# Attention and gated FFN on one core: the order of TensorE, ScalarE and VectorE taken from a list schedule

## The chip, the core and the metric

The kernel runs on one core of a Trainium2 chip. The core has TensorE (PE: matrix products, into the eight banks of PSUM), ScalarE (ACT: exponential, tanh, copies), VectorE (DVE: elementwise work and copies), GpSimd (POOL, here only the issuer of the loads) and SyncE (SP, here the issuer of the first small loads and of the stores). Each engine takes its instructions in the order in which the program gives them to it and waits at semaphores for the others. The metric is the device time of one execution in microseconds, lower is better.

## The reference

Sparse attention over 4 batches, 8 heads, 768 positions and a head size of 64, followed by a gated feed-forward network (512 to 1536 to 512) over the 3072 tokens, whose rows `x` are the heads' results side by side:

```python
    scores = scale * np.matmul(q, k.transpose(0, 1, 3, 2))
...
    mask = np.abs(blk_i - blk_j) <= window
    mask = mask | (blk_i == 0) | (blk_j == 0) | (blk_i == n_blocks - 1) | (blk_j == n_blocks - 1)
...
    scores = np.where(mask, scores, -1000000000.0)
    scores = scores - np.max(scores, axis=-1, keepdims=True)
    attn = np.exp(scores)
    attn = attn / (np.sum(attn, axis=-1, keepdims=True) + 1e-09)
    return np.matmul(attn, v).astype(np.float32)
...
    gate = 1.0 / (1.0 + np.exp(-(x @ w_gate)))
    val = x @ w_val
    return (gate * val @ w_out).astype(np.float32)
```

The mask is in blocks of 32 positions; three further blocks in each row of blocks come from the input `sampled_blocks`.

## The kernel before

A **unit** is one batch `b` with 256 of its 768 query positions (`u` = 0 to 2); there are 12, `n` = 0 to 11. A unit has four **pairs** of heads (`p`) and each pair three **steps** (`j`), of 256 key positions each. A step is `qk` (four score matmuls into `st`, two PSUM banks), `exp` on ACT (`pt<-st`, line 235) and `mul` on DVE with the 0/1 mask (line 239). After three steps a pair's `pv` multiplies with v, extended by a column of ones, so that the row sums come along (24 matmuls, line 257); `norm` divides by them on DVE (lines 267 and 269, giving `x16`), and `xt` transposes the result on PE and copies it into `xT` (lines 279 and 282).

The FFN of a unit has 12 column blocks `f`: eight matmuls into one bank `pg` (gate and value, line 295), tanh on ACT (`th`, line 305) and the gate on DVE (`ht`, line 306). Then `y` multiplies `ht` with `w_out`, 12 matmuls for each half of the unit (`py`, line 323), ACT copies the result to SBUF (line 332) and SP stores it.

A batch must be prepared: k, q and v are loaded in 16 bits (`k16`, `q16`, `v16`, two buffers each, for even and odd batches) by DMAs that POOL issues. For each pair and each of k and q, `pair_copy` gathers the two heads on DVE (`pr`, line 188), `pair_turn` transposes on PE (`tpq`, line 197) and copies into `kT` or `qT` (lines 202 and 204); `vcopy` copies v into `vex` (line 207).

All order is written out by hand: the main loop, from line 438, gives each unit six slots (`sl`), and a slot two steps. Slots 2 to 5 carry three `f` blocks each of the FFN of unit n−1, slots 0 and 1 the two `y` halves of unit n−2. `extra_copy` at a slot's end and `extra_pe` in the next slot put in one copy and one transpose of the next batch, from its list `pairs`, which is filled in each batch's second unit. Unit 0 has a loop of its own (from line 401), step by step, without an FFN. PSUM's eight banks are two score buffers of two banks and four single banks under the tag `m`, handed out in turn.

Of the kernel before, what the change touches and what calls it, by code (L numbers as in the profile page):

```python
# [14 lines left out]
ALU = mybir.AluOpType  # L16
# [13 lines left out]
NU = S // UQ  # L30

# [5 lines left out]
def _det_block_mask() -> np.ndarray:  # L37
    qb = np.arange(NB)[:, None]
    kb = np.arange(NB)[None, :]
    m = (np.abs(qb - kb) <= 1) | (qb == 0) | (kb == 0) | (qb == NB - 1) | (kb == NB - 1)  # L40
    return m.astype(np.float32)


@with_exitstack
def kernel(
# [87 lines left out]
    for j in range(3):  # L133
        load_wo(j)
    for r in range(2):
        nc.vector.memset(vex[r][:, :, :, D : D + 1], 1.0)
# [5 lines left out]
    def mask_blocks():  # L142
# [14 lines left out]
    def mask_rows():  # L157
        for c0, c1 in ((0, 512), (512, S)):
            p24 = ps.tile([NB, 512], f32, tag="m", bufs=4, name="p24")
            nc.tensor.matmul(  # L160
                p24[:, 0 : c1 - c0], mb16, e24[:, c0:c1], start=True, stop=True
            )
            nc.vector.tensor_copy(mb24[:, c0:c1], p24[:, 0 : c1 - c0])

    def mask_tile(c0, c1, t, eng):
        n = c1 - c0
        pm = ps.tile([128, 512], f32, tag="m", bufs=4, name="pm")
        w = 512 // n
        for i in range(w):
            nc.tensor.matmul(  # L170
                pm[:, i * n : (i + 1) * n],
                e24[:, (t + i) * 128 : (t + i + 1) * 128],
                mb24[:, c0:c1],
# [3 lines left out]
        dst = mask[:, t : t + w, c0:c1]  # L177
        src = pm.rearrange("a (w n) -> a w n", w=w)
        if eng is nc.scalar:
            nc.scalar.copy(dst, src)  # L180
        else:
            nc.vector.tensor_copy(dst, src)


    def pair_copy(src, b, p, t0=0, t1=NT):

        pr = work.tile([128, NT, 2, D], f16, tag="pr", bufs=4, name="pr")
        nc.vector.tensor_copy(  # L188
            pr[:, t0:t1, :, :],
            src[b % 2][:, 2 * p : 2 * p + 2, t0:t1, :].rearrange("a h t d -> a t h d"),  # L190
        )
        return pr

    def pair_turn(pr, dst, b, p, t0=0, t1=NT, eng=None):
        tp = ps.tile([128, 1024], f16, tag="m", bufs=4, name="tpq")
        for t in range(t0, t1):
            nc.tensor.transpose(  # L197
                tp[:, (t - t0) * 128 : (t - t0 + 1) * 128], pr[:, t, :, :], ident
            )
        d_ = dst[b % 2][:, p, t0 * 128 : t1 * 128]  # L200
        if eng is nc.scalar:
            nc.scalar.copy(d_, tp[:, 0 : (t1 - t0) * 128])  # L202
        else:
            nc.vector.tensor_copy(d_, tp[:, 0 : (t1 - t0) * 128])  # L204

    def vcopy(b, p):
        nc.vector.tensor_copy(
            vex[b % 2][:, 2 * p : 2 * p + 2, :, 0:D],
            v16[b % 2][:, 2 * p : 2 * p + 2, :, :],
        )  # L210

    class Step:


        def __init__(self, b, u, p, j):
            self.b, self.u, self.p, self.j = b, u, p, j

        def qk(self):
            b, u, p = self.b, self.u, self.p
            self.st = ps.tile([128, 2, 2, UQ], f32, tag="s", bufs=2, name="st")  # L220
            for i in range(2):
                t = 2 * self.j + i
                for a in range(2):
                    o = a * D
                    nc.tensor.matmul(  # L225
                        self.st[:, a, i, :],
# [6 lines left out]
        def exp(self):  # L233
            self.pt = work.tile([128, 2, 2, UQ], f16, tag="P", bufs=12, name="pt")
            nc.scalar.activation(self.pt, self.st, AF.Exp, bias=0.0, scale=SCALE)  # L235

        def mul(self):
# [8 lines left out]
    class Pair:  # L246


        def __init__(self, b, u, p, steps, xT):
            self.b, self.u, self.p, self.steps, self.xT = b, u, p, steps, xT  # L250

        def pv(self):
# [268 lines left out]
```

## Time and profile before

| | |
|---|---|
| time, median of 3 runs | 344.76 us (344.62 to 345.37) |
| the profiled execution | 344.88 us, span of its profile 343.1 us |
| ACT | 210.3 us busy, 323 instructions |
| DVE | 220.4 us busy, 531 instructions |
| loads issued by POOL | 14.16 MB as written, in 27.6% of the DMA engines' time over the span |

The page of a profile gives the busy time of each engine, the span in slices, the chain of work that ended last, and groups of instructions by line. Below, rows of the page's groups read: line, engine, operation, what it writes and reads, shapes, count, then busy microseconds and mean nanoseconds of one, then the idle time just before them and what ended it. Rows of an engine's timeline read: start and length in microseconds, engine, line, operation, count, and in brackets how long the engine had sat idle before and what it waited for. Rows of windows read: the stretch, its length, busy microseconds (and instructions) of PE, PE's weight loads, DVE, ACT and POOL, the granted clock of PE, the mean busy share of the DMA engines, and GB/s.

### The profile page before, as it was taken

The page shows a single profiled execution, that of the slowest core. Times are in us where ns is not written, and L with a number is a line of the kernel's source. Part 1 is how long each engine was busy: PE and PEld are TensorE (multiplying, and loading weights), DVE is VectorE, ACT ScalarE, POOL GpSimd, SP SyncE. Part 2 cuts the span into 40 slices and gives each one's busy share as a digit, 9 for nine tenths or more (in the row PEclk, how much of TensorE's full clock was granted, in tenths as well). Part 3 has the DMA queues.
Part 4 walks back from the last instruction along what each step waited for, and adds up shares of the span by engine and source line. Part 5 has one row for each costly group of instructions (what it writes and reads, how often), then busy time and mean ns, then how long its engine had stood idle before and what let it go on. Part 6 is the DMA issues. An engine that isn't in the chain of part 4 may idle for free.

```text
span 343.1 us, 8102 instructions
## 1 busy us (share of the span) xinstructions
PE 308.3 (90%) x3470; PEld 221.2 (64%) x3470; DVE 220.4 (64%) x531; ACT 210.3 (61%) x323; POOL 26.0 (8%) x37
## 2 busy tenths in 40 slices
PE   2788459899999999899999998999999999999995
PEld 1234237666858757657858766758768768678682
DVE  3655635777766757776767767767757757667240
ACT  1656325556867765656767856557867778677241
POOL 8834200003000000000000000000000000000000
PEclk9999658999999999999999999999999999999999
DMA  8999999509900000000000010000010010000101
GB/s 98 187 202 204 206 204 204 88 3 172 168 31 32 3 31 32 2 32 33 0 32 33 2 61 2 2 32 33 0 60 6 2 61 2 31 34 3 61 2 61
DMA packets 23215, 21.03 MB, mean 61 GB/s; under 512 B 2164, under 2 KB 20108, under 8 KB 23180
## 3 DMA queue, kind: packets, MB, share of 16 engines
q0 software_dynamic: 19472, 14.16, 27.6%
q1 hardware_dynamic: 3708, 6.37, 5.0%
q8 instruction: 27, 0.44, 0.5%
q14 instruction: 8, 0.07, 0.1%
HBM read 28.39 MB, written 6.29 MB: 101 GB/s over the span
## 4 chain that ended last, share of the span: by engine, by line
PE 76%; DMA 12%; DVE 6%; ACT 2%; POOL 2%; issue 1%; POOLq 0%
PE pg L295 36%; PE py L323 18%; PE pv L257 10%; PE st L225 6%; DMA q<-in_q_dram 6%; DMA wg<-in_moe_w_gate_dram 4%; PE tpq L197 3%; DVE pr L188 2%; DMA k<-in_k_dram 2%; DVE ht L306 2%; PE tpx L279 1%; DVE xT L282 1%; ACT pt L235 1%; ACT th L305 1%; DVE pt L239 1%
## 5 line engine op out<-in xcount | busy, mean ns | idle before, releaser
L235 ACT ACTIVATE pt<-st 128x1024 f16<-128x1024 f32 x144 | 144.5, 1022 | 14.4 <-PE st L225 13.1
L239 DVE TENSOR_TENSOR pt<-pt,mask 128x1024 f16<-128x1024 f16 x144 | 99.1, 690 | 49.1 <-ACT pt L235 49.0
L305 ACT ACTIVATE th<-pg 128x256 f32<-128x256 f32 x144 | 55.4, 385 | 59.1 <-PE pg L295 57.0
L295 PE MATMUL pg<-xT,wg 128*128 128x256 f16 x576 | 87.5, 275 | 0.0
L295 PE MATMUL pg<-xT,wv 128*128 128x256 f16 x576 | 87.0, 274 | 0.0
L323 PE MATMUL py<-wo,ht 128*128 128x512 f16 x288 | 67.6, 379 | 0.0
L306 DVE SCALAR_TENSOR_TENSOR ht<-th,pg 128x256 f16<-128x256 f32 x144 | 59.0, 416 | 10.8 <-ACT th L305 9.0
L295 PEld LDWEIGHTS <-wv 128*128 128x128 f16 x576 | 56.7, 99 | 6.9
L295 PEld LDWEIGHTS <-wg 128*128 128x128 f16 x576 | 51.5, 98 | 11.4 <-issue 4.4
L225 PE MATMUL st<-qT,kT 64*128 64x256 f16 x576 | 48.6, 286 | 4.3 <-ACT qT L202 4.1
L257 PEld LDWEIGHTS <-pt 128*128 128x128 f16 x1152 | 45.6, 101 | 4.7 <-issue 1.0
L257 PE MATMUL pv<-vex,pt 128*128 128x65 f16 x1152 | 47.6, 199 | 0.4 <-DVE pt L239 0.4
L323 PEld LDWEIGHTS <-ht 128*128 128x128 f16 x288 | 26.1, 98 | 28.8 <-issue 2.5
L197 PE MATMUL tpq<-ident,pr 128*128 128x128 f16 x192 | 19.7, 244 | 25.6 <-DVE pr L188 23.5
L332 ACT ACTIVATE ysb<-py 128x512 f32<-128x512 f32 x24 | 14.3, 597 | 42.1 <-PE py L323 42.1
L197 PEld LDWEIGHTS <-pr 128*128 128x128 f16 x192 | 12.4, 107 | 36.3 <-DVE pr L188 34.2
L225 PEld LDWEIGHTS <-kT 64*128 64x128 f16 x576 | 22.6, 96 | 18.4 <-issue 12.3
L282 DVE COPY xT<-tpx 128x256 f16<-128x256 f16 x48 | 13.8, 288 | 14.1 <-PE tpx L279 14.1
L269 DVE TENSOR_TENSOR x<-pv,rz 128x256 f16<-128x256 f32 x48 | 20.4, 425 | 1.7
L204 DVE COPY kT<-tpq 128x768 f16<-128x768 f16 x16 | 8.9, 558 | 10.4 <-PE tpq L197 10.4
L279 PE MATMUL tpx<-ident,x 128*128 128x128 f16 x96 | 13.7, 226 | 0.1
L279 PEld LDWEIGHTS <-x 128*128 128x128 f16 x96 | 9.1, 99 | 7.1 <-issue 1.2
(29 smaller groups left out, 79.9 us busy)
## 6 DMA issues: line engine op xcount, KB each, us to landing
out_dram<-ysb SPq DMA_DIRECT2D x24, 256.0 KB, 2.0
k<-in_k_dram POOLq DMA_DIRECT2D x3, 768.0 KB, 18.3
q<-in_q_dram POOLq DMA_DIRECT2D x3, 768.0 KB, 20.9
v<-in_v_dram POOLq DMA_DIRECT2D x3, 768.0 KB, 22.8
wg<-in_moe_w_gate_dram POOLq DMA_DIRECT2D x4, 384.0 KB, 12.4
wv<-in_moe_w_val_dram POOLq DMA_DIRECT2D x4, 384.0 KB, 14.1
wo<-in_moe_w_out_dram POOLq DMA_DIRECT2D x3, 512.0 KB, 16.9
k<-in_k_dram POOLq DMA_DIRECT2D x4, 192.0 KB, 6.2
```

What stands on the lines that cost most here:

```text
L197: nc.tensor.transpose(tp[:, (t - t0) * 128 : (t - t0 + 1) * 128], pr[:, t, :, :], ident)
L225: nc.tensor.matmul(self.st[:, a, i, :], kT[b % 2][o : o + D, p, t * 128 : (t + 1) * 128], qT[b % 2][o : o + D, p, u * UQ : (u + 1) * UQ], ...
L235: nc.scalar.activation(self.pt, self.st, AF.Exp, bias=0.0, scale=SCALE)
L239: nc.vector.tensor_tensor(self.pt, self.pt, m.unsqueeze(1).broadcast_to([128, 2, 2, UQ]), op=ALU.mult,)
L257: nc.tensor.matmul(self.acc[:, s, a, :], self.steps[t // 2].pt[:, a, t % 2, s * 128 : (s + 1) * 128], vex[self.b % 2][:, 2 * self.p + a, t ...
L269: nc.vector.tensor_tensor(self.x16, self.acc[:, :, :, 0:D], rz.broadcast_to([128, 2, 2, D]), op=ALU.mult,)
L279: nc.tensor.transpose(tp[:, s * 128 : (s + 1) * 128], self.x16[:, s, :, :], ident)
L282: nc.vector.tensor_copy(self.xT[:, self.p, :], tp[:, 0:UQ])
L295: nc.tensor.matmul(self.pg[:, i, :], w[:, c, f * 128 : (f + 1) * 128], self.xT[:, c, :], start=(c == 0), stop=(c == 3),)
L305: nc.scalar.activation(th, self.pg[:, 0, :], AF.Tanh, bias=0.0, scale=0.5)
L306: nc.vector.scalar_tensor_tensor(self.ht[:, f, :], in0=th, scalar=1.0, in1=self.pg[:, 1, :], op0=ALU.add, op1=ALU.mult,)
L323: nc.tensor.matmul(self.py, self.ht[:, f, s * 128 : (s + 1) * 128], wo[:, f, :], start=(f == 0), stop=(f == NF - 1),)
```

## The change

The instructions stay nearly the same, and so do the tiles and the arithmetic. What is new is that the program first builds a list of **tasks** (a block of matmuls, an exponential, a copy) with the engines that may run each, a duration for each engine, the tasks that it depends on, an earliest time (`at`) from a reckoning of when each load lands (`land`, with `DMA_RATE`), and the PSUM banks that it takes and frees. `Plan.run` plays this list through in modelled time: whenever an engine is free it starts the first task of the list that is ready and for which a bank is there. The instructions are then given to the engines in the order of these starts, and each task gets the bank that the plan gave it (`spare`, four single banks `m0` to `m3`; `score`, two buffers `s0` and `s1`).

Copies out of PSUM may go to ACT or DVE, whichever is free. Rings are larger: `P` 15 buffers instead of 12, `xT` 4 instead of 3, `th`, `x16` and `ysb` 4 instead of 3. The `y` blocks are no longer cut in two. Loads of batch 1 are issued by the program right behind the weights; those of batches 2 and 3 by a task of their own (`later`), with 16 us from its issue to its landing. The order of DMAs in POOL's queue and of stores in SP's is the same as before.

```diff
+PE, ACT, DVE, DMA = "PE", "ACT", "DVE", "DMA"
+DMA_RATE = 0.385
+XB, PB, VB = 4, 4, 5
...
+class Plan:
+    LAG = {PE: 0.25, ACT: 0.06, DVE: 0.06, DMA: 16.0}
+    def __init__(self, banks):
+        self.tasks = []
+        self.room = {kind: [(0.0, i) for i in range(n)] for kind, n in banks.items()}
+    def add(self, engines, fn, deps=(), at=0.0, take=(), free=()):
+        self.tasks.append((engines, fn, list(deps), at, list(take), list(free)))
+        return len(self.tasks) - 1
+    def run(self):
+        n = len(self.tasks)
+        left = [len(set(t[2])) for t in self.tasks]
+        after = [[] for _ in range(n)]
+        for i, t in enumerate(self.tasks):
+            for d in set(t[2]):
+                after[d].append(i)
+        ready = sorted(i for i in range(n) if not left[i])
+        busy = {PE: 0.0, ACT: 0.0, DVE: 0.0, DMA: 0.0}
+        events = [(0.0, -1)] + [(t[3], -1) for t in self.tasks if t[3] > 0]
+        heapq.heapify(events)
+        order, end = [], 0.0
+        while events:
+            now, i = heapq.heappop(events)
+            if i >= 0:
+                for bank in self.tasks[i][5]:
+                    self.room[bank.kind].append((now, bank.slot))
+                for j in after[i]:
+                    left[j] -= 1
+                    if not left[j]:
+                        bisect.insort(ready, j)
+            if events and events[0][0] <= now:
+                continue
+            for eng in busy:
+                if busy[eng] > now:
+                    continue
+                for j in ready:
+                    engines, fn, _, at, take, _ = self.tasks[j]
+                    cost = dict(engines).get(eng)
+                    if cost is None or at > now:
+                        continue
+                    kinds = [bank.kind for bank in take]
+                    if any(len(self.room[x]) < kinds.count(x) for x in kinds):
+                        continue
+                    for bank in take:
+                        oldest = min(self.room[bank.kind])
+                        self.room[bank.kind].remove(oldest)
+                        bank.slot = oldest[1]
+                    ready.remove(j)
+                    busy[eng] = now + cost
+                    heapq.heappush(events, (now + cost, -1))
+                    heapq.heappush(events, (now + cost + self.LAG[eng], j))
+                    order.append((eng, fn))
+                    end = max(end, now + cost)
+                    break
+        assert len(order) == n
+        for eng, fn in order:
+            fn(eng)
+        return end
...
+    for dst, src in ((k16, k), (q16, q), (v16, v)):
+        load_heads(dst, src, 1, 0, H)
...
+    plan = Plan({'m': 4, 's': 2})
+    spare = [ps.tile([128, 512], f32, name=f"m{i}") for i in range(4)]
+    score = [ps.tile([128, 2, 2, UQ], f32, name=f"s{i}") for i in range(2)]
...
+    landed = 3.9
+    land = {}
+    for p in range(NP):
+        for nm, mb in (("k", 0.393), ("q", 0.131), ("v", 0.393)):
+            landed += mb / DMA_RATE
+            land[nm, p] = landed
+    for nm, mb in (("w", 0), ("q2", None), ("w", 1), ("w", 2), ("w", 3)):
+        landed += (1.05 if mb is None else 1.573) / DMA_RATE
+        land[nm, mb] = landed
+    for j in range(3):
+        landed += 1.05 / DMA_RATE
+        land["wo", j] = landed
+    for nm in "kqv":
+        landed += 1.573 / DMA_RATE
+        land[nm, "next"] = landed
...
+        n = t1 - t0
+        a = plan.add([(DVE, 0.15 + 0.035 * n)], pair, ring("pr", PB) + loaded[b], at=at)
+        copies[b].append(a)
+        c = plan.add([(PE, 0.058 * n)], turn, [a], take=[bank])
+        used["pr"].append(c)
+        return plan.add(
+            [(DVE, 0.14 + 0.07 * n), (ACT, 0.18 + 0.1 * n)], evac, [c] + deps, free=[bank]
...
+        deps = [x for pr, st in run for x in (kdone[pr.b, pr.p], qdone[pr.b, pr.p, pr.u])]
+        a = plan.add([(PE, 0.1 + 0.22 * len(run))], mm, deps, take=[st.bank for pr, st in run])
+        for pr, st in run:
+            read["qk", pr.b, pr.p] = [a]
+            i = NP * pr.n + pr.p - VB
+            old = [used["P"][i]] if i >= 0 else []
+            e = plan.add([(ACT, 0.98)], st.exp, [a] + old, free=[st.bank])
+            pr.products.append(plan.add([(DVE, 0.66)], st.mul, [e] + masks[st.j, st.u]))
...
+            deps = xdone[self.n] + (ring("ht", 2) if f == 0 else [])
+            a = plan.add([(PE, 0.88)], mm, deps, at=land["w", f // 3], take=[bank])
+            if f == NF - 1:
+                used["xT"].append(a)
+            c = plan.add([(ACT, 0.36)], tanh, [a] + ring("th", 4))
+            g = plan.add([(DVE, 0.41)], gate, [c], free=[bank])
+            used["th"].append(g)
+            self.gated.append(g)
...
+            a = plan.add([(PE, 2.6)], mm, self.gated, at=land["wo", 2], take=[bank])
+            if s == 1:
+                used["ht"].append(a)
+            plan.add([(ACT, 0.6), (DVE, 0.69)], evac, [a], free=[bank])
...
+    def later(b):
+        if b > 1:
+            def load(eng):
+                for src, dst in ((k, k16), (q, q16), (v, v16)):
+                    load_heads(dst, src, b, 0, H)
+            loaded[b].append(plan.add([(DMA, 0.01)], load, copies[b - 2]))
+        for p in range(NP):
+            for nm, fn in (("k", prep_k), ("q", prep_q), ("v", prep_v)):
+                preps.append(
+                    lambda fn=fn, p=p, at=land[nm, "next"] if b == 1 else 0.0: fn(b, p, at)
+                )
...
-        if u == 0 and b + 1 < B:
-            for src, dst in ((k, k16), (q, q16), (v, v16)):
-                load_heads(dst, src, b + 1, 0, H)
-        if u == 1 and b + 1 < B:
-            for p in range(NP):
-                for src, dst in ((k16, kT), (q16, qT)):
-                    pairs.append((src, dst, b + 1, p, 0, NT))
...
-            sa.qk()
-            if n > 1 or sl > 1:
-                sb.qk()
-            sa.exp()
-            extra_pe()
-            sa.mul()
...
+            if n == 1:
+                for x in run:
+                    scores([x])
+            else:
+                scores(run)
             if sl >= 2:
-                if sl == 2:
-                    ffn[n - 1] = Ffn(*units[n - 1], xTs[n - 1])
-                F = ffn[n - 1]
-                fs = [3 * (sl - 2) + i for i in range(3)]
+                for i in range(3):
+                    ffn[n - 1].f(3 * (sl - 2) + i)
+                    if i == 0 and sl % 3 != 1:
+                        do(valued, do_value)
             elif n > 1:
-                F = ffn[n - 2]
-            if sl >= 2:
-                F.f(fs[0])
-            elif F:
-                F.y(sl, 0, 6)
-            sb.exp()
-            sb.mul()
-            if sl % 3 in (0, 2):
-                value()
-            if sl >= 2:
-                F.f(fs[1])
-                F.f(fs[2])
-            elif F:
-                F.y(sl, 6, NF)
-            if sl % 3 in (0, 1):
-                xts()
-            extra_copy()
-            for p, j in pair:
-                if j == 2:
-                    waiting.append(Pair(*units[n], p, steps[p], xTs[n]))
-    F = ffn[-2]
-    xts()
-    value()
-    F.y(0, 0, NF)
-    xts()
-    F.y(1, 0, NF)
-    F = Ffn(*units[-1], xTs[-1])
+                ffn[n - 2].y(sl)
+            if sl == 0:
+                do(valued, do_value)
+            if sl % 3 != 2:
+                do(turned, Pair.xt)
+            if u > 0:
+                do(preps, lambda fn: fn())
```

Three places show what the plan makes of it. The first is **ACT at the start**. Before: the first copy of q, then unit 0's exponentials, with the mask's casts among them.

```order
L62 ACT_TABLE_LOAD
L202 COPY qT0_81<-tpq_135 128x256
L235 ACTIVATE pt_156<-st_151 128x1024
L235 ACTIVATE pt_185<-st_158 128x1024
L235 ACTIVATE pt_198<-st_187 128x1024
L202 COPY qT0_81<-tpq_200 128x256
L235 ACTIVATE pt_214<-st_204 128x1024
L235 ACTIVATE pt_234<-st_216 128x1024
L180 CAST mask_69<-pm_242 128x512
```

Of the change (`copy` is line 222, `exp` line 391):

```order
L138 ACT_TABLE_LOAD
L222 CAST mb24_121<-m0_122 24x512
L222 COPY kT0_83<-m2_124 128x768
L222 CAST mask_69<-m0_122 128x2x256
L222 CAST mask_69<-m3_125 128x2x256
L391 ACTIVATE pt_187<-s0_126 128x1024
L391 ACTIVATE pt_196<-s1_127 128x1024
L391 ACTIVATE pt_210<-s0_126 128x1024
L391 ACTIVATE pt_219<-s1_127 128x1024
L391 ACTIVATE pt_227<-s0_126 128x1024
L391 ACTIVATE pt_237<-s1_127 128x1024
L222 CAST mask_69<-m1_123 128x512
```

Four copies now stand ahead of the first exponential, and six exponentials follow one another.

The second is **ACT in a slot with FFN blocks**, of a middle unit. Before:

```order
L235 ACTIVATE pt_809<-st_799 128x1024
L305 ACTIVATE th_829<-pg_820 128x256
L235 ACTIVATE pt_832<-st_804 128x1024
L305 ACTIVATE th_873<-pg_864 128x256
L305 ACTIVATE th_885<-pg_876 128x256
```

Of the change (tanh is line 516):

```order
L391 ACTIVATE pt_1025<-s0_126 128x1024
L391 ACTIVATE pt_1053<-s1_127 128x1024
L516 ACTIVATE th_1068<-m0_122 128x256
L516 ACTIVATE th_1079<-m3_125 128x256
L516 ACTIVATE th_1093<-m2_124 128x256
```

The second exponential moved ahead of the first tanh.

The third is **DVE where the next batches are prepared**. Before, in unit 1 (the names end in 1 for batch 1): batch 1's first copies stand ahead of unit 1's products (line 239).

```order
L188 COPY pr_512<-k16_1_76 128x768
L204 COPY kT1_84<-tpq_521 128x768
L239 TENSOR_TENSOR pt_519<-pt_519,mask_69 128x1024
L239 TENSOR_TENSOR pt_535<-pt_535,mask_69 128x1024
L282 COPY xT_119<-tpx_538 128x256
L188 COPY pr_542<-q16_1_74 128x768
L204 COPY qT1_82<-tpq_556 128x768
L207 COPY vex1_80<-v16_1_78 128x12x64
L239 TENSOR_TENSOR pt_554<-pt_554,mask_69 128x1024
```

Of the change, in unit 2, behind all of batch 1's copies (`k_0`, `q_0` and `v_0` are batch 2's now; `DMASW` in the brackets is a wait for a load; products are line 397, gates line 521, normalizations lines 430 and 432):

```order
L326 COPY pr<-k_0_75 128x768 [waits DMASW3_49,DVE_49]
L430 RECIPROCAL rz<-m_122 128x4 [waits PE_49]
L432 TENSOR_TENSOR x_977<-m_122,rz 128x256 [waits DVE_49]
L397 TENSOR_TENSOR pt<-pt,mask 128x1024 [waits Activation_49]
L326 COPY pr<-q_0_73 128x768 [waits DMASW4_49]
L397 TENSOR_TENSOR pt<-pt,mask 128x1024 [waits Activation_49]
L521 SCALAR_TENSOR_TENSOR ht<-th,m_123 128x256 [waits Activation_49]
L521 SCALAR_TENSOR_TENSOR ht<-th,m_125 128x256 [waits Activation_49]
L521 SCALAR_TENSOR_TENSOR ht<-th,m_124 128x256 [waits Activation_49]
L359 COPY vex_79<-v_0_77 128x12x64 [waits DMASW5_49]
L397 TENSOR_TENSOR pt<-pt,mask 128x1024 [waits Activation_49]
```

Batch 1's copies moved behind unit 1's last product, and the first copies of batch 2 moved up from unit 4 into unit 2, each with a wait for its load.

433 lines of the change are left out of this document (245 added, 188 removed).

## The prediction

> **What bounds the kernel now.** I read the page first, for the balance of the engines.
>
> ```profile
> span 343.1 us, 8102 instructions
> PE 308.3 (90%) x3470; PEld 221.2 (64%) x3470; DVE 220.4 (64%) x531; ACT 210.3 (61%) x323; POOL 26.0 (8%) x37
> ```
>
> TensorE (PE) is the busiest, but a share says nothing of where it is full. The chain that ended last, in order of time, does: the first down-projection (`py`) of each unit marks the passage from unit to unit (columns: start, length, what).
>
> ```profile
> 72.74 1.29 PE py L323 x6
> ...
> 96.75 1.40 PE py L323 x6
> ...
> 119.83 1.40 PE py L323 x6
> ...
> 148.57 1.29 PE py L323 x6
> ...
> 172.58 1.40 PE py L323 x6
> ...
> 195.67 1.40 PE py L323 x6
> ...
> 224.41 1.29 PE py L323 x6
> ...
> 248.41 1.40 PE py L323 x6
> ```
>
> The distances are 24.0, 23.1, 28.7, 24.0, 23.1, 28.7 and 24.0 us. The 23.1 units hold no transposes of the next batch, the 24.0 units two and the 28.7 units six. PE's timeline inside a 23.1 unit, here one of its six slots, shows no idle brackets (they would stand at the row's end with what ended the wait):
>
> ```profile
> 255.82 0.61 PE L295 MATMUL pg<-xT,wg 128*128 128x256 f16 x4
> ...
> 256.70 0.93 PE L257 MATMUL pv<-vex,pt 128*128 128x65 f16 x24
> 257.47 0.60 PE L295 MATMUL pg<-xT,wg 128*128 128x256 f16 x4
> ...
> 259.86 0.61 PE L295 MATMUL pg<-xT,wg 128*128 128x256 f16 x4
> ```
>
> Every start is the end of the issue before it: eight `pg` 0.88, 24 `pv` 0.77, two more `pg` blocks and the next scores 2.39. No order of these instructions shortens a 23.1 unit much. What can be won lies in the transposes and ahead of unit 2, whose first scores start at 70.96. PE's timeline there:
>
> ```profile
> 20.81 1.50 PE L257 MATMUL pv<-vex,pt 128*128 128x65 f16 x24
> ...
> 28.01 0.61 PE L225 MATMUL st<-qT,kT 64*128 64x256 f16 x4 [1.54 <-ACT qT L202]
> ...
> 45.97 0.82 PE L197 MATMUL tpq<-ident,pr 128*128 128x128 f16 x6 [6.19 <-DVE pr L188]
> ...
> 50.48 1.06 PE L295 MATMUL pg<-xT,wg 128*128 128x256 f16 x4
> ...
> 54.96 0.60 PE L295 MATMUL pg<-xT,wg 128*128 128x256 f16 x4
> ...
> 57.20 0.51 PE L197 MATMUL tpq<-ident,pr 128*128 128x128 f16 x6 [0.66 <-DVE pr L188]
> 57.54 0.60 PE L295 MATMUL pg<-xT,wg 128*128 128x256 f16 x4
> ...
> 58.41 0.94 PE L257 MATMUL pv<-vex,pt 128*128 128x65 f16 x24
> ...
> 70.96 0.61 PE L225 MATMUL st<-qT,kT 64*128 64x256 f16 x8
> ```
>
> Unit 0's scores go one by one with waits, then PE sits for 6.2 us at 45.97, and the gated FFN begins only at 50.48. VectorE's timeline says why: its queue runs in order, and its next copies in line are of batch 1, which had not landed.
>
> ```profile
> 45.56 0.36 DVE L188 COPY pr<-k 128x768 f16<-128x768 f16 x1 [5.17 <-DMA k<-in_k_dram]
> ...
> 49.45 0.36 DVE L188 COPY pr<-q 128x768 f16<-128x768 f16 x1
> ...
> 53.28 0.37 DVE L207 COPY vex<-v 128x768 f16<-128x768 f16 x1 [1.99 <-DMA v<-in_v_dram]
> ```
>
> Batch 1 lands at 45.5, 49.4 and 53.3. The work of unit 1, ready since long before, stands behind those copies.
>
> **The change, part by part.** *Start.* The copies of batch 1 now stand behind all of unit 1's products on VectorE, so they hold nothing back until about 45. What paces the start then is ScalarE (ACT). Its groups and its rows at the start:
>
> ```profile
> L235 ACT ACTIVATE pt<-st 128x1024 f16<-128x1024 f32 x144 | 144.5, 1022 | 14.4 <-PE st L225 13.1
> L239 DVE TENSOR_TENSOR pt<-pt,mask 128x1024 f16<-128x1024 f16 x144 | 99.1, 690 | 49.1 <-ACT pt L235 49.0
> L305 ACT ACTIVATE th<-pg 128x256 f32<-128x256 f32 x144 | 55.4, 385 | 59.1 <-PE pg L295 57.0
> L306 DVE SCALAR_TENSOR_TENSOR ht<-th,pg 128x256 f16<-128x256 f32 x144 | 59.0, 416 | 10.8 <-ACT th L305 9.0
> ```
>
> ```profile
> 8.68 1.94 ACT L235 ACTIVATE pt<-st 128x1024 f16<-128x1024 f32 x2 [0.70 <-PE st L225]
> ...
> 18.44 0.59 ACT L180 CAST mask<-pm 128x512 f16<-128x512 f32 x1 [1.99 <-PE pm L170]
> ...
> 32.49 1.97 ACT L235 ACTIVATE pt<-st 128x1024 f16<-128x1024 f32 x2
> ```
>
> Two exponentials in a row take 1.94. From its first exponential to the last of unit 1, ACT's new queue holds 24 exponentials (about 24.0 us), 9 tanh (3.4), 5 mask casts of 0.59 (2.9) and 5 small copies (estimated 0.38 each from the tanh, of the same 256 columns: 1.9), 32.2 in all. A cast, a 768-wide copy and two mask casts now stand ahead of the first exponential, so I put it at 9.5 instead of 8.68. Walking the new queues of PE, ACT and VectorE against each other with the durations above, ACT waits some 5 us on the way: about 1 while PE turns the second pair, 2 around the three mask casts that hold PSUM banks `m1`, `m3`, `m0`, 1 before the third pair's last scores, 1 later. That ends the last exponential of unit 1 at 46.7. PE has one `pg` block to finish, so unit 2's first scores start at about 47.7.
>
> The clock adds to it. A block of 24 `pv` took 1.50 at 20.81 and 0.94 at 58.41, four `pg` 1.06 at 50.48 and 0.60 at 54.96: PE runs at half speed there, though the window at 28 still shows a granted clock of 1.00 (the number ahead of the DMA share and the GB/s).
>
> ```profile
> 28.00:32.00 4.00, 3.99 (x38) 2.14 (x37) 1.41 (x4) 1.37 (x2) 1.95 (x3) 1.00 1.31 203
> ...
> 40.00:44.00 4.00, 0.00 (x0) 0.00 (x0) 0.39 (x2) 0.85 (x1) 0.00 (x0) 0.50 1.31 204
> ```
>
> Four microseconds of continuous FFN brought full speed by 54.96, so the new FFN start, at about 32, loses between 0 and 2 us; I take 0.8. Unit 2 starts at **48.5**, instead of 70.96: 22.5 won. (The Trainium skill, "TensorE: Matmul & The Clock Gate", Part 1, says that the array starts at half clock and gets the full one after some 3.4 us of sustained work. The trace agrees for 50.48 to 54.96. By the rule the new order, which I see dense on PE from about 17, would be at full clock well ahead of 32 and lose nothing: the sum would be 0.8 lower.)
>
> *Transposes.* From unit 2 on, 19 of them remain now. They cost 0.9 in each of the units of 24.0 (three) and 5.65 in those of 28.7 (two), 14.0, and the one at the start of unit 2 about 1.0. In the new order the copies `pr` run several transposes ahead, on VectorE's idle time, so each costs only its issue, 0.34 (57.20 to the next `pg` at 57.54). But all 8 of batch 1 now fall behind unit 2's start: 24 × 0.34 = 8.2. Won: 15.0 − 8.2 = 6.8.
>
> *Loads of batch 2.* These are the new stall. The DMA queue keeps its order, and VectorE's queue now has a copy of batch 2's k, then of q, then of v, in unit 2 already (earlier: unit 4). The constant in the plan gives a load 16 us from its issue. The windows show the DMA engines full until nearly 64:
>
> ```profile
> 63.00:64.00 1.00, 1.00 (x12) 0.90 (x10) 0.96 (x3) 0.09 (x1) 0.00 (x0) 1.00 0.85 124
> 64.00:65.00 1.00, 1.00 (x11) 0.90 (x10) 0.80 (x2) 1.00 (x2) 0.00 (x0) 1.00 0.14 20
> ```
>
> Behind batch 1's v at 53.3, at 3.85 apiece less a little, k lands at about 57, q at 60.5 and v at 63.9. With unit 2 from 48.5, VectorE comes to these copies at about 59, 61 and 63: k costs nothing, q nothing or 0.5, v about 1. Behind the v copy stand two products, a normalization and gates, and PE's next `x` transpose waits for that normalization. I take 0.8 us; 0 if unit 2 starts 2 us later, 6 if it starts at 45 or earlier, when all three are waited for. Batch 3's loads wait for VectorE's copies of batch 1, which end near 58 instead of 78; nothing needs them before unit 5.
>
> *Steady units.* ACT now does both exponentials ahead of the three tanh. In the old order one tanh stood between:
>
> ```profile
> 255.76 1.02 ACT L235 ACTIVATE pt<-st 128x1024 f16<-128x1024 f32 x1
> 256.90 0.38 ACT L305 ACTIVATE th<-pg 128x256 f32<-128x256 f32 x1
> 257.19 1.02 ACT L235 ACTIVATE pt<-st 128x1024 f16<-128x1024 f32 x1
> ```
>
> The first `pg` bank of a slot is so held about 1 us longer. Does PE wait? In the quoted slot `pg` starts at 255.82 and the exponentials at 255.76; the next slot's first `pg`, which often gets the same bank, starts at 259.86. Two exponentials end 1.94 later, at 257.7, the tanh at 258.1; with a product (0.69) and, as an estimate, as much for a normalization ahead of it on VectorE, the gate (0.42) ends between 258.5 and 259.5. The slack is 0.4 or more, which an `xT` copy, now sometimes on ACT, can eat. I take 1.5 us over the ten units, between 0 (the bank is always free) and the full 1.02 in each of 40 slots, near the lower end because of that slack.
>
> *Evacuations moved from VectorE to ACT* (16 of `xT`, 6 of 768 columns) cost about 10 us of ACT and are hidden: 220 of 315 us. *The tail* is the same sequence, 0.
>
> **The sum**, against the profiled execution (span 343.1, time 344.88, so 1.8 outside; the median 344.76 is 0.1 away): 343.1 − 22.5 − 6.8 + 0.8 + 1.5 = 316.1, + 1.8 = **317.9 us**.
>
> **The rivals.**
> 1. *The start does worse.* The plan's exponential is 0.98 and its clock always full, the rows say 1.02 and half. If every hand-over in the three queues costs more, ACT waits 12 instead of 5 and unit 2 starts at 56: 325. For it: half clock until 54 in the trace. Against it: banks and products are ready early.
> 2. *The order of ACT shifts the wait to PSUM banks.* If PE loses 0.3 in each of the 40 slots, 12 − 1.5 more: 328. Against it: the slack of 0.4.
> 3. *Slower than before.* The same mechanism at its full price: each first gate of a slot 1.02 later and nothing takes it up, 40 × 1.02 = 41 against 29.3 won: about 356. It decides from 0.73 lost per slot; the slack speaks against it.
> 4. *The change does nothing.* If batch 1's loads set unit 2's start after all (copies at 53.3 needed first), PE would start it at about 70 as now, and only the transposes count: 338. Against it: the new order has unit 1's exponentials and gates ahead of every batch 1 copy.
> 5. *Better.* Full clock from 20 and few waits: unit 2 at 46, no lost bank: 313.
>
> **How the numbers follow.** Forecast (312 to 322) 0.55, rival 5 within it; rival 1 0.2; rival 2 0.15; rival 4 and mishaps of its size 0.05; rival 3 0.03, a plain draw 0.02. To leave out no more than 0.2 the range goes from 311 to 328. Faster by over 0.2% (what a measurement here can tell from no change) 0.95, within it 0.02, slower 0.03.
>
> **What would show it.** Right: PE's first scores of unit 2 near 48.5; no wait of `pg` for batch 1's copies; VectorE waits for batch 2's q or v between 59 and 64 of under 2 us in all; transposes followed by the next matmul after 0.34; free units of 23.1. Wrong: repeated `PE <- DVE ht` waits in the steady slots (rival 2 or 3), unit 2's scores after 53 (rival 1), a stall of over 3 us at batch 2's copies (unit 2 was early, and the load takes over as the bound).

## The result, and the profile after

The changed kernel took **316.96 us** (median of 4 runs, 316.68 to 317.23) against 344.69 for the kernel before in the same comparison (344.08 to 345.37): a ratio of 0.9195, interval 0.9175 to 0.9215. The profiled execution took 317.23 us, its span is 315.4, so 27.7 below the 343.1 of before. Lines of the page of after, the last two from its chain that ended last:

```profile
span 315.4 us, 8130 instructions
...
PE 299.3 (95%) x3470; PEld 217.6 (69%) x3470; DVE 214.1 (68%) x510; ACT 214.1 (68%) x344; POOL 25.9 (8%) x37
...
PE 77%; DMA 19%; POOL 1%; DVE 1%; issue 1%; ACT 0%; POOLq 0%
PE m L505 36%; PE m L544 18%; DMA v<-in_v_dram 11%; PE m L420 10%; PE s L381 9%; DMA wo<-in_moe_w_out_dram 5%; DMA wv<-in_moe_w_val_dram 3%; PE m L335 2%; PE m L441 1%; POOL k L175 0%; POOL q L175 0%; DVE pt L397 0%; POOL v L175 0%; ACT ysb L555 0%; DVE x L432 0%
```

TensorE is now 95% busy with the same 3470 matmuls. The chain passes through a load of batch 2's v for 29.9 us (36.62 to 66.49), most of the 11% shown. This is a new wait, but not one of that size, since PE works during most of the load. (In the changed file all PSUM banks read `m`; L381 are the scores, L391 the exponentials, L420 `pv`, L505 `pg`, L521 the gates, L544 `y`, L326 the copies `pr`, L335 the transposes `tpq`, L359 the copies of v, L432 the normalization.)

PE's timeline of after up to unit 2, whose first scores stand in the last row:

```profile
19.46 1.53 PE L420 MATMUL m<-vex,pt 128*128 128x65 f16 x24
...
21.78 0.45 PE L381 MATMUL s<-qT,kT 64*128 64x256 f16 x4
...
26.24 0.95 PE L420 MATMUL m<-vex,pt 128*128 128x65 f16 x24
...
31.10 0.61 PE L505 MATMUL m<-xT,wg 128*128 128x256 f16 x4
...
47.03 0.61 PE L381 MATMUL s<-qT,kT 64*128 64x256 f16 x8
```

Unit 2 starts at 47.03 instead of 70.96, and the FFN at 31.10 already runs at full speed. The copies that VectorE had waited for in the middle of unit 1's work are gone from there. In their place stand three rows some 13 us further on, of batch 2 (VectorE's timeline of after):

```profile
58.11 0.36 DVE L326 COPY pr<-k 128x768 f16<-128x768 f16 x1 [0.99 <-DMA k<-in_k_dram]
...
62.65 0.36 DVE L326 COPY pr<-q 128x768 f16<-128x768 f16 x1 [3.03 <-DMA q<-in_q_dram]
...
66.51 0.36 DVE L359 COPY vex<-v 128x768 f16<-128x768 f16 x1 [1.91 <-DMA v<-in_v_dram]
```

What stands behind them on VectorE comes late, a gate for `pv` and a normalization for `tpx`. PE's timeline there shows its only two waits after 47, 3.25 us together:

```profile
61.55 0.60 PE L505 MATMUL m<-xT,wv 128*128 128x256 f16 x4
63.99 0.93 PE L420 MATMUL m<-vex,pt 128*128 128x65 f16 x24 [1.85 <-DVE ht L521]
...
68.07 0.27 PE L441 MATMUL m<-ident,x 128*128 128x128 f16 x2 [1.40 <-DVE x L432]
...
69.00 0.49 PE L335 MATMUL m<-ident,pr 128*128 128x128 f16 x6
69.33 0.60 PE L505 MATMUL m<-xT,wg 128*128 128x256 f16 x4
```

From there on the chain of after runs through PE. Its `y` blocks mark the units 3 to 8:

```profile
78.48 2.59 PE m L544 x12
...
101.45 2.59 PE m L544 x12
...
125.55 2.59 PE m L544 x12
...
150.43 2.59 PE m L544 x12
...
173.41 2.59 PE m L544 x12
...
197.51 2.59 PE m L544 x12
```

The distances are 23.0, 24.1, 24.9, 23.0 and 24.1, where before had 23.1, 28.7, 24.0, 23.1 and 28.7: the 28.7 us units are gone. A slot of a unit without transposes, in PE's timeline of after, is as full as it was:

```profile
255.60 0.61 PE L505 MATMUL m<-xT,wg 128*128 128x256 f16 x4
...
256.48 0.94 PE L420 MATMUL m<-vex,pt 128*128 128x65 f16 x24
257.26 0.60 PE L505 MATMUL m<-xT,wg 128*128 128x256 f16 x4
...
259.75 0.61 PE L505 MATMUL m<-xT,wg 128*128 128x256 f16 x4
```

No row has a bracket, and 255.60 to 259.75 is 4.15 us against 4.04 in the slot shown of before, which had no `tpx` in it (two of them cost 0.2).

The balance of the 27.7 us by PE's first instruction of each stage: up to unit 2's first scores −23.9 (70.96 to 47.03); from there to unit 3's first `y` +5.6 (25.7 before, 31.3 after: 3.25 of waits, 0.8 for one `pv` block, the rest transposes that stood elsewhere before); from unit 3 to unit 11 −8.2 (197.85 to 189.65); from unit 11's first `y` to the end −1.1. The `pv` block, 0.77 us, stands ahead of a unit's first `y` in after and behind it in before, so at the end it is missing again and 0.4 of the 1.1 is left.

### The profile page after: what moved, and what is told of

Its sections match the earlier page's. It is cut to its first block, busy times and chain, and to the rows that moved or that the text cites. A ratio compares the mean times of both kernels' runs of the same rounds, so it can differ in the third digit from the quotient of the medians.

```text
span 315.4 us, 8130 instructions
## 1 busy us (share of the span) xinstructions
PE 299.3 (95%) x3470; PEld 217.6 (69%) x3470; DVE 214.1 (68%) x510; ACT 214.1 (68%) x344; POOL 25.9 (8%) x37
## 4 chain that ended last, share of the span: by engine, by line
PE 77%; DMA 19%; POOL 1%; DVE 1%; issue 1%; ACT 0%; POOLq 0%
PE m L505 36%; PE m L544 18%; DMA v<-in_v_dram 11%; PE m L420 10%; PE s L381 9%; DMA wo<-in_moe_w_out_dram 5%; DMA wv<-in_moe_w_val_dram 3%; PE m L335 2%; PE m L441 1%; POOL k L175 0%; POOL q L175 0%; DVE pt L397 0%; POOL v L175 0%; ACT ysb L555 0%; DVE x L432 0%
## 5 line engine op out<-in xcount | busy, mean ns | idle before, releaser
L391 ACT ACTIVATE pt<-s 128x1024 f16<-128x1024 f32 x144 | 140.2, 1027 | 7.0 <-PE s L381 6.3
L516 ACT ACTIVATE th<-m 128x256 f32<-128x256 f32 x144 | 55.1, 389 | 49.4 <-PE m L505 42.3
L505 PE MATMUL m<-xT,wg 128*128 128x256 f16 x576 | 86.7, 273 | 0.0
L505 PE MATMUL m<-xT,wv 128*128 128x256 f16 x576 | 86.4, 273 | 0.0
L521 DVE SCALAR_TENSOR_TENSOR ht<-th,m 128x256 f16<-128x256 f32 x144 | 56.9, 416 | 16.4 <-ACT th L516 15.2
L544 PE MATMUL m<-wo,ht 128*128 128x512 f16 x288 | 66.0, 379 | 0.0
L505 PEld LDWEIGHTS <-wv 128*128 128x128 f16 x576 | 56.4, 98 | 6.5
L505 PEld LDWEIGHTS <-wg 128*128 128x128 f16 x576 | 51.4, 98 | 11.1 <-issue 5.9
L420 PE MATMUL m<-vex,pt 128*128 128x65 f16 x1152 | 46.4, 196 | 3.6 <-DVE ht L521 1.8
L420 PEld LDWEIGHTS <-pt 128*128 128x128 f16 x1152 | 42.9, 99 | 8.9 <-issue 6.9
L544 PEld LDWEIGHTS <-ht 128*128 128x128 f16 x288 | 26.7, 98 | 30.5 <-issue 1.9
L381 PE MATMUL s<-qT,kT 64*128 64x256 f16 x576 | 46.9, 279 | 0.6 <-DVE qT L224 0.3
L381 PEld LDWEIGHTS <-kT 64*128 64x128 f16 x576 | 22.0, 95 | 15.9 <-issue 8.6
L432 DVE TENSOR_TENSOR x<-m,rz 128x256 f16<-128x256 f32 x48 | 20.4, 424 | 1.7
L335 PE MATMUL m<-ident,pr 128*128 128x128 f16 x192 | 17.1, 231 | 1.0 <-DVE kT L224 0.5
L335 PEld LDWEIGHTS <-pr 128*128 128x128 f16 x192 | 12.4, 103 | 5.5 <-issue 3.1
```

Source lines behind the costliest of these rows:

```text
L335: nc.tensor.transpose(m16(bank.slot)[:, (t - t0) * 128 : (t - t0 + 1) * 128], box[0][:, t, :, :], ident,)
L381: nc.tensor.matmul(score[self.bank.slot][:, a, i, :], kT[b % 2][o : o + D, p, t * 128 : (t + 1) * 128], qT[b % 2][o : o + D, p, u * UQ : ( ...
L391: nc.scalar.activation(self.pt, score[self.bank.slot], AF.Exp, bias=0.0, scale=SCALE)
L420: nc.tensor.matmul(self.acc[:, s, a, :], self.steps[t // 2].pt[:, a, t % 2, s * 128 : (s + 1) * 128], vex[self.b % 2][:, 2 * self.p + a, t ...
L432: nc.vector.tensor_tensor(self.x16, self.acc[:, :, :, 0:D], rz.broadcast_to([128, 2, 2, D]), op=ALU.mult,)
L505: nc.tensor.matmul(pg[:, i, :], w[:, c, f * 128 : (f + 1) * 128], xTs[self.n][0][:, c, :], start=(c == 0), stop=(c == 3),)
```

## The experiments

Theory A is the prediction's: VectorE's queue runs in order, so a copy that waits for a load holds back all work behind it; the list schedule gains by standing those copies behind the ready work, and by having each `pr` copied well ahead of its transpose. "Ratio" is to the kernel before.

| run | median us (lowest to highest) | ratio (interval) |
|---|---|---|
| before_late | 336.44 (336.07 to 336.90) | 0.9762 (0.9745 to 0.9780) |
| before_ahead | 336.75 (336.59 to 337.87) | 0.9773 (0.9752 to 0.9794) |
| before_both | 325.33 (324.76 to 325.57) | 0.9433 (0.9417 to 0.9449) |
| both_mask | 323.56 (321.56 to 324.35) | 0.9357 (0.9313 to 0.9401) |
| at1_28 | 330.82 (329.97 to 331.50) | 0.9600 (0.9581 to 0.9620) |
| at1zero | 363.28 (363.18 to 363.75) | 1.0548 (1.0532 to 1.0564) |
| at2 | 314.23 (313.86 to 315.49) | 0.9128 (0.9104 to 0.9151) |
| at2_warm | 313.68 (313.31 to 313.94) | 0.9100 (0.9086 to 0.9113) |
| b3late | 317.30 (317.02 to 317.35) | 0.9209 (0.9195 to 0.9222) |
| store_late | 317.33 (317.16 to 317.88) | 0.9205 (0.9190 to 0.9220) |
| store_late2 | 315.78 (315.43 to 315.91) | 0.9160 (0.9146 to 0.9173) |
| dveonly | 317.24 (316.68 to 318.26) | 0.9203 (0.9182 to 0.9225) |

### The place of batch 1's copies

**before_late** does this one thing in the kernel before, by hand: batch 1's preparation begins in unit 2 instead of unit 1, two copies and two transposes in each slot.

```diff
-        if u == 1 and b + 1 < B:
+        if u == (2 if b == 0 else 1) and b + 1 < B:
...
             extra_copy()
+            if n == 2:
+                extra_copy()
+                extra_pe()
```

> The kernel before, by hand, with only batch 1's preparation moved from unit 1 to unit 2 (two copies and two transposes in a slot). My theory: PE's wait of 6.2 us at 45.97 and the smaller ones behind it go, FFN starts near 42, unit 2 near 60, and unit 2 gets 4 to 6 us longer by the transposes: 335 to 339. Rival (unit 0's step by step order is the whole loss): 342 to 345.

336.44. Unit 0's `y` starts at 58.50 instead of 72.74 (−14.2), and unit 2, which now holds the whole preparation, takes 30.2 us instead of 24.0 (+6.2): −8.0 by the profile.

**at1_28** undoes it in the changed kernel: batch 1's copies count as ready at 28 us, and the plan puts them where VectorE has a gap then.

```diff
-                    lambda fn=fn, p=p, at=land[nm, "next"] if b == 1 else 0.0: fn(b, p, at)
+                    lambda fn=fn, p=p, at=28.0 if b == 1 else 0.0: fn(b, p, at)
```

> The changed kernel with the plan told that batch 1 lands at 28 us (it lands at 45.5, 49.4 and 53.3); unlike the run with 0, v's copies then stand behind unit 0. My theory: VectorE reaches batch 1's k near 31 and stands until 45.5, then until 49.4 (q) and 53.3 (v) with unit 1's products and gates behind it; unit 2 starts at 61 to 65 and the time is 326 to 332. Rival (the wait of the run with 0 cost so much only because it stood ahead of everything; here unit 1's work would hide it): 317 to 321.

330.82. In VectorE's timeline of at1_28 the waits for batch 1 are back:

```profile
45.12 0.36 DVE L326 COPY pr<-k 128x768 f16<-128x768 f16 x1 [13.41 <-DMA k<-in_k_dram]
...
48.98 0.36 DVE L326 COPY pr<-q 128x768 f16<-128x768 f16 x1 [2.30 <-DMA q<-in_q_dram]
```

Unit 2's first scores start at 64.86 instead of 47.03, 17.8 later; 13.9 of it is left in the time.

**at1zero** ran before at1_28 and was meant to do the same, with `at=0.0` for every batch.

> The changed kernel with the plan told that batch 1 is there from the beginning (its earliest times are 0); nothing else. VectorE's queue then has batch 1's first copy behind row 57, ahead of unit 1's products, as the kernel before had. My theory (the start was won by taking these waits out of VectorE's queue): VectorE stands from about 29 to 45.5 and again until 49.4, unit 2's first scores move from 47 to 63 to 66, batch 2's waits vanish, and the time is 328 to 334. Rival (the start was won by packing unit 0's exponentials and by free choice of the copying engine): 317 to 321.

363.28, slower than before by 5%. The direction held, the size missed by some 30 us, since the edit was stronger than I had seen: with no earliest time the plan put batch 1's v ahead of nearly everything on VectorE, the first copies of batch 0 included (VectorE's timeline of at1zero):

```profile
52.44 1.17 DVE L359 COPY vex<-v 128x768 f16<-128x768 f16 x4 [51.15 <-DMA v<-in_v_dram]
53.52 0.15 DVE L228 CAST sbf<-sbi 24x3 f32<-24x3 uint16 x1
```

The same tiles and the same planner, with one wrong number in it, cost 46 us against after.

### Batch 2's loads

**at2** gives batch 2's copies the time at which the trace of after shows the loads landing, in place of 16 us from their issue.

```diff
+    late = {("k", 2): 59.0, ("q", 2): 63.5, ("v", 2): 67.0}
...
-                    lambda fn=fn, p=p, at=land[nm, "next"] if b == 1 else 0.0: fn(b, p, at)
+                    lambda fn=fn, p=p, at=land[nm, "next"] if b == 1 else late.get((nm, b), 0.0): fn(b, p, at)
```

> The changed kernel, with one more line in the plan: the copies of batch 2 may not be placed before 59 (k), 63.5 (q) and 67 us (v) of the plan's time, which is about when the trace shows them landing (58.1, 62.6, 66.5). My theory: VectorE's waits of 1.0, 3.0 and 1.9 us on these loads cost PE the two gaps of 1.85 and 1.40 us, so 317.0 becomes 313.5 to 314.5 and unit 2 shows no PE gap over 0.5 us. Rival: the copies are then late for unit 3 and the wait moves to their transposes; then within 1 us of 317.

314.23, 2.7 us under after: faster than both kernels. PE's timeline of at2 at the place of the gaps:

```profile
61.97 0.60 PE L505 MATMUL m<-xT,wv 128*128 128x256 f16 x4
62.40 0.94 PE L420 MATMUL m<-vex,pt 128*128 128x65 f16 x24
...
64.92 0.28 PE L441 MATMUL m<-ident,x 128*128 128x128 f16 x2
65.13 0.61 PE L381 MATMUL s<-qT,kT 64*128 64x256 f16 x8
```

No bracket is left from 47 to 80, and unit 3's first `y` starts at 75.00 (after: 78.31). The stall is the price of an estimate in the plan, not of the hardware.

Why do the loads land 1 to 2.6 us later than I had reckoned? **b3late** holds back batch 3's loads, which after issues at 53 to 58, until 89: a one-column copy of unit 2's `ht` on POOL stands ahead of them.

```diff
+                if b == 3:
+                    hold = sing.tile([128, 1], f16, name="hold")
+                    nc.gpsimd.tensor_copy(hold, ffn[2].ht[:, 0, 0:1])
```

> The changed kernel with batch 3's loads held back on POOL until the FFN of unit 2 has its first gate (near 86 us instead of 53 to 58); a copy of one column on POOL does the waiting. It asks why batch 2's v landed at 66.5 and not at 63.9. If the output stores of unit 0 (256 KB each, at 52 and 56) share the DMA engines: v still at 66 to 66.8, time 316.5 to 317.5. If batch 3's loads take the share: v at 63.9 to 64.5, PE's gaps 2 us less, 314.5 to 315.5.

317.30, as after. Without any load of batch 3 in the queue v's copy still starts at 66.32 (66.51): not the cause.

The other suspects are unit 0's two output stores, at 56 to 62. **store_late** put them behind unit 1's in the program text.

```diff
+                held.append((self.b, 2 * self.u + s, ysb))
+                if self.n > 0 and not (self.n == 1 and s == 0):
+                    for hb, ht, hy in held:
+                        nc.sync.dma_start(
```

> The changed kernel with unit 0's two stores issued only behind unit 1's second store. If the stores of 256 KB take the DMA engines from batch 2's loads: VectorE gets q at 60.3 to 61.2 and v at 63.7 to 64.5, PE's two gaps shrink to about 1 us together, 314.5 to 315.7. If they do not: q 62.6, v 66.5 and 317 as in the changed kernel.

317.33, but no verdict: SP's queue kept its old order, and the stores went out as before (v's copy starts at 66.42). **store_late2** then puts unit 1's second store first in SP's queue, so that unit 0's wait behind it until 83.5.

```diff
-                    for hb, ht, hy in held:
+                    for hb, ht, hy in reversed(held):
```

> The late stores once more, now with unit 1's second store first in SP's queue, so that unit 0's stores really go out near 82 us (in the first try the queue's order, and so the time of the stores, was unchanged). If the stores take the DMA engines from batch 2's loads: VectorE gets q at 60.3 to 61.5 and v at 63.7 to 64.8, 314.5 to 315.7. If not: v still near 66.5 and 317.

315.78, a little above what was expected of the theory. Two windows of after, with the DMA share and GB/s last, show the stores as a higher rate:

```profile
56.00:58.00 2.00, 2.00 (x43) 1.65 (x42) 1.05 (x4) 1.82 (x3) 0.85 (x2) 1.00 1.22 260
...
60.00:62.00 2.00, 2.00 (x22) 1.41 (x21) 0.00 (x0) 1.50 (x4) 0.00 (x0) 1.00 1.22 260
```

In the same windows of store_late2 they are gone:

```profile
56.00:58.00 2.00, 2.00 (x43) 1.61 (x41) 1.43 (x4) 2.00 (x4) 0.87 (x1) 1.00 1.31 204
...
60.00:62.00 2.00, 1.85 (x20) 1.16 (x18) 0.81 (x2) 1.57 (x3) 0.00 (x0) 1.00 1.32 204
```

and q and v come 1.4 us earlier than in after (VectorE's timeline of store_late2):

```profile
61.19 0.36 DVE L327 COPY pr<-q 128x768 f16<-128x768 f16 x1 [1.90 <-DMA q<-in_q_dram]
...
65.08 0.36 DVE L360 COPY vex<-v 128x768 f16<-128x768 f16 x1 [1.93 <-DMA v<-in_v_dram]
```

So the stores make up 1.4 of the 2.6 us by which v was later than predicted. Another 0.9 lies in the reckoning itself: three loads at 3.85 us apiece behind batch 1's v at 53.28 end at 64.8, not at the 63.9 of the prediction. The rows here are 3.89 us apart and those of at1_28 3.86, so there was no "little" to take off. The last 0.3 stays open.

### The transposes

**before_ahead** lets the transposes of batches 2 and 3 in the kernel before run one slot later, so that each `pr` is copied a slot ahead of its transpose.

```diff
-        if copied:
+        if copied and (len(copied) > 1 or not pairs or copied[0][2] < 2):
```

> The kernel before, by hand, with the transposes of batches 2 and 3 one slot later behind their copies, so that a copy is always one slot ahead. My theory: the 0.7 to 0.9 us waits of these transposes go, the units of 28.7 become 25.2 to 26, in all 5 to 7 us: 337.5 to 339.5. Rival (the wait only moves to the copy out of PSUM or to the scores behind): 342 to 345.

336.75, 8.0 us under before, a little better than expected. A slot of the old 28.7 us unit, in PE's timeline of before, and under it the same slot of before_ahead:

```profile
131.76 0.61 PE L225 MATMUL st<-qT,kT 64*128 64x256 f16 x8
133.03 0.51 PE L197 MATMUL tpq<-ident,pr 128*128 128x128 f16 x6 [0.66 <-DVE pr L188]
133.38 0.60 PE L295 MATMUL pg<-xT,wg 128*128 128x256 f16 x4
```

```profile
130.55 0.61 PE L225 MATMUL st<-qT,kT 64*128 64x256 f16 x8
131.10 0.51 PE L197 MATMUL tpq<-ident,pr 128*128 128x128 f16 x6
131.44 0.60 PE L295 MATMUL pg<-xT,wg 128*128 128x256 f16 x4
```

The transpose now follows the scores at once and costs its issue, 0.34. The 28.7 us units take 24.9, the same as in after.

**before_both** joins this, for all batches, with before_late.

> The kernel before with both hand edits: batch 1's preparation in unit 2, and in all batches the copies one slot ahead of their transposes. If the two causes are separate, the gains add (7.9 and 8.0 us), and unit 2, which had become 6 us longer by transposes that wait, gets 3 to 4 of these back: 323 to 327. What is left to 317 is then unit 0's packing by the plan. If they overlap: 329 to 334.

325.33, 19.3 under before's 344.67 in that comparison, where before_late alone had −7.9 and before_ahead −8.0. They more than add up, since the transposes that before_late crowds into unit 2 are the ones that copying ahead makes cheap (unit 2 takes 27.5, not 30.2). Two hand edits give 70% of the list schedule's gain. Unit 2's first scores start at 57.12; in after at 47.03.

### What is left: unit 0

**both_mask** is before_both, and the six mask casts that only units 1 and 2 need move from the middle of unit 0 to its last three steps.

```diff
-        if 3 <= s < 9:
-            mask_tile(UQ, S, s - 3, nc.scalar)
+        if s >= 9:
+            mask_tile(UQ, S, 2 * (s - 9), nc.scalar)
+            mask_tile(UQ, S, 2 * (s - 9) + 1, nc.scalar)
```

> The two hand edits once more, and with them the six mask casts for units 1 and 2 moved to the last three steps of unit 0, so that ACT's exponentials of unit 0 are no longer behind casts that wait for PE (2.0, 2.7 and 2.7 us of waiting in the run with both edits). If this packing of unit 0 is what the plan won beyond the two edits: exponentials close up, unit 2's first scores move from 57.1 to 53 to 55.5, 321.0 to 323.5. If ACT only waits for something else instead (scores behind the copies of q, which also pass through ACT): 324.5 to 326.

323.56, just above the range of the one theory and below the rival's. Its runs spread over 2.8 us; the spans (323.8 and 322.5) and the start of unit 2 (57.12 and 55.88) put the gain at 1.2 to 1.3. So the casts are a part of it, and a small one. Most of the 8.9 us between 55.88 and 47.03 was not taken apart. The traces name one suspect, PE's speed: in both_mask a `pv` at 36.05 still takes 1.50 instead of 0.94, where after has full speed from 21.8. The larger rings weren't tried alone; from unit 3 to unit 11 they can matter little, for before_both, without them, takes 190.1 us there and after 189.65.

**dveonly** keeps the list schedule, but lets only VectorE copy into `xT`, `kT` and `qT`.

```diff
-            [(DVE, 0.14 + 0.07 * n), (ACT, 0.18 + 0.1 * n)], evac, [c] + deps, free=[bank]
+            [(DVE, 0.14 + 0.07 * n)], evac, [c] + deps, free=[bank]
...
-                plan.add([(DVE, 0.29), (ACT, 0.37)], self.evac, [c] + deps,
+                plan.add([(DVE, 0.29)], self.evac, [c] + deps,
```

> The changed kernel with the copies into xT, kT and qT on VectorE alone, planned anew. My theory (moving them was neither price nor gain in the full units, and matters little at the start, where ACT and VectorE are both three quarters full): 317 to 320, with units 3 to 10 as long as in the changed kernel. Rival (the free choice of engine is what frees PSUM banks in time): above 324, with waits of PE for VectorE in the steady slots.

317.24, as after, but not by the same way: unit 2's first scores start at 48.90, 1.9 later, and unit 3's first `y` at 77.33, 1.0 earlier, because a later unit 2 meets the loads of batch 2 with only one wait (1.32 for v). So the plan with the free choice of engine is 1.9 us ahead at the start, and the load stall takes it back; with at2's better landing times it might count, which wasn't run. How much of the 1.9 is the copies themselves isn't shown, because PE's speed differs too (PE's timeline of dveonly, and a window):

```profile
14.96 0.94 PE L420 MATMUL m<-vex,pt 128*128 128x65 f16 x24
...
19.50 1.50 PE L420 MATMUL m<-vex,pt 128*128 128x65 f16 x24
```

```profile
20.00:24.00 4.00, 4.00 (x40) 2.19 (x38) 2.06 (x6) 2.39 (x4) 0.74 (x1) 0.50 1.34 203
```

PE was at full speed from 14.65, fell back to half speed at 18.23 and stayed there until about 28, where after is at full speed from 21.8.

**at2_warm** is at2 with eight 128x512 matmuls on zeros at the very start of PE, to have full speed from the first scores on.

```diff
+    for _ in range(8):
+        nc.tensor.matmul(score[0][:, 0, :, :], wt[:, 0:128], wt, start=True, stop=True)
```

> The run at2 with eight matmuls of 128x512 on zeros ahead of everything on PE (from about 1.4 to 5 us, while it has nothing to do; they add work whose result nothing reads). It asks what the half clock of the start costs. If PE's speed paces the start: full speed well before 21 us, unit 2's first scores 0.8 to 1.5 us earlier than in at2, 312.8 to 313.5. If ACT's queue paces it: pv at 18 us no longer 1.5 us long, but unit 2 within 0.4 us of at2, 313.9 to 314.5.

313.68; the interval overlaps at2's. It did not do what it was for (PE's timeline of at2_warm):

```profile
1.19 3.59 PE L249 MATMUL s<-wt 128*128 128x512 f16 x8 [1.19 <-DVE wt L214]
...
17.83 1.48 PE L425 MATMUL m<-vex,pt 128*128 128x65 f16 x24 [1.59 <-ACT mask L224]
...
23.84 0.39 PE L386 MATMUL s<-qT,kT 64*128 64x256 f16 x4
```

`pv` at 17.83 still takes 1.48, and full speed comes between 23.4 and 23.8. In other runs with the same first 20 us of PE's order it comes between 20.8 (at1_28) and 23.4 (b3late; after: 21.8), so the zeros brought nothing forward, and that they held it back isn't shown. Unit 2 starts at 47.45, as in at2. What half speed costs the start stays open.

## Why the prediction was right

*What bounds the kernel: right, and shown from both sides.* Moving batch 1's copies back into the changed kernel brings the wait and 13.9 us (at1_28), at their worst 46 (at1zero); moving them away in the kernel before wins 7.9, and with the copies ahead of the transposes 19.3. It is not the whole of the start: with both hand edits unit 2 begins at 57.12, so 10.1 of the 23.9 us were won elsewhere in units 0 and 1. The mask casts explain 1.2 of these; the cause of the rest stays open.

*The start: right in size, −23.9 for −22.5.* ScalarE's rows of after give the first exponential, predicted at 9.5, and the last of unit 1, predicted to end at 46.7:

```profile
9.44 1.94 ACT L391 ACTIVATE pt<-s 128x1024 f16<-128x1024 f32 x2
...
43.56 1.96 ACT L391 ACTIVATE pt<-s 128x1024 f16<-128x1024 f32 x2
```

It ended at 45.52, 1.2 earlier than predicted, though not by shorter waits: between 9.44 and 45.52 ACT was busy for 29.9 of 36.1 us, so it stood 6.1 us instead of my 5, and its instructions, which overlap a little, took 2.3 less than the 32.2 of the sum. Nor did ACT pace the start to its end: PE's timeline of after shows no bracket from 28.75 to 61.55, so from there on PE was the pace. The clock term was mis-sized: I put 0.8 on the half-speed FFN, and the `pg` at 31.10 takes 0.61, full speed, so 0. The granted clock reads 1.00 in the windows of after even ahead of 21.8, where PE's rows are at half speed, and only the durations show it. (By the rule of the Trainium skill, "TensorE: Matmul & The Clock Gate", Part 1, that some 3.4 us of sustained work bring the full clock, this term would be 0, and for the dense work of after from 17.97 to 21.78 the trace agrees. at2_warm disagrees: there PE was busy for 7.00 of the 7.00 us from 9 to 16, and half-speed rows go on until 23.4.)

*The transposes: right.* They won 8.2 from unit 3 to unit 11 and gave back 1.5 in unit 2, where batch 1's now stand (5.6 less 3.25 of waits and the `pv` block): −6.7 against a predicted −6.8. before_ahead shows the mechanism alone, and each transpose is followed after 0.34.

*The loads of batch 2: right mechanism, the mis-sized term.* "Unit 2 from 48.5 … I take 0.8 us; 0 if unit 2 starts 2 us later, 6 if it starts at 45 or earlier". VectorE waited 5.9 us and PE 3.25, shown by at2, which wins 2.7 by moving the copies alone. Two steps made it too small: unit 2 came at 47.03, and the loads ended at 58.1, 62.6 and 66.5, not at 57, 60.5 and 63.9. "At 3.85 apiece less a little" left out the output stores, which share the DMA engines and explain 1.4 of v's 2.6 us; the "little" itself is 0.9 more.

*The steady bank waits: 1.5 predicted, none found.* From 69 us on the chain runs through PE, and PE's timeline shows no bracket from there to the end. The slack of 0.4 held; rivals 2 and 3 had no place, nor had rival 1. Rival 5 (unit 2 at 46, no lost bank, 313) came near, but for batch 2's stall: at2, without it, takes 314.23. ACT's extra copies were hidden, as predicted; without them the start is 1.9 us longer (dveonly), in part perhaps by PE's speed. *The tail* was 0.4 us shorter, not 0, when the `pv` block is left aside.

So −23.9 − 6.7 + 3.25 − 0.4 gives the −27.7, rounding aside, where the forecast was −27.0. Part of that closeness is luck: the start came out 1.4 better, the bank waits 1.5 and the tail 0.4, the transposes 0.1 worse and the stall 2.5.

## What to carry to other kernels

In an in-order queue, look for an instruction that waits for a load while work stands ready behind it: its price can be the whole wait, for every engine that this queue feeds (at1_28: VectorE stood 17.4 us for batch 1, and unit 2 came 17.8 later), or about half of it where the others still have work (after: 5.9 and 3.25). A planner with durations removes such waits as well as its landing times are true: take them from a trace, stores included, and plan again; here that was worth 2.7 us more, and one missing time cost 46. When an engine that paced the start gets faster, the next load becomes the pace, so an improvement ahead of it can be worth nothing (dveonly) until the load is seen to.

## What was unexpected of the hardware

PE ran at half speed with a granted clock of 1.00 in the windows at the start of before, of after and of at2_warm; in dveonly, after it had once been at full speed and fallen back, the windows do read 0.50. When half speed ends isn't plain. Back-to-back matmuls on zeros (1.19 to 4.78) and dense work from 9 to 16 did not end it in at2_warm, while dense work of the same kinds from 8.50 to 14.65 did in dveonly. In after and the runs with its start it ended 3 to 6 us behind the start of the first `pv`. Whether the data, the shapes or the short pauses matter wasn't tried. And two stores of 256 KB, at a higher total rate (260 against 204 GB/s), delayed loads issued before them by 1.4 us.
